# New order tables for a fused RWKV and WaveMLP kernel: r of two pairs loaded first, weight casts in groups of three, all bonus products on GpSimd

## The chip, the cores and the metric

The kernel runs on one core of a Trainium2 chip. The metric is device time in microseconds (us) of one launch, taken as the median of several runs. Beside it stands one profiled execution, from which all durations of single instructions come.

## The reference, cut to what matters

Two stages follow each other. The first is a recurrent attention over 4 batches, 8 heads, 768 tokens and a head size of 48, with a decay `w` and a bonus `u` per head and channel. The second is a mixing block over the 384 channels.

```
for t in range(S):                                # attention, per batch and head
    cur = einsum('bhd,bhe->bhde', u * k_t, v_t)
    y_t = einsum('bhd,bhde->bhe', r_t, state + cur)
    state = w * state + einsum('bhd,bhe->bhde', k_t, v_t)
x = y, heads side by side                         # 4 x 768 x 384
theta = x @ w_theta
z_r, z_i = x * cos(theta), x * sin(theta)
u = x + w_tok_r @ z_r + w_tok_i @ z_i             # over the 768 tokens
out = u + max(u @ w_ch, 0)
```

## The kernel before

The attention is done in pairs of chunks of 128 tokens: 3 pairs per batch, 12 pairs in all, called g0 to g11 here (`g` in the code). The pairs g0 to g6 are loaded token by token in pairs of neighbours (one DMA each for k, r and v), the later ones in two halves for k and v.

For each pair these steps follow each other:

- SP loads k, r and v as float32 (`load`, DMA at L476, halves at L482), into a ring of 16 buffers `ld`.
- The decay products `Kw` and `Rw` (L613, for later pairs L615) multiply k and r with tables of powers of w. The tables are made by ACT at L429 in the opening.
- PE turns both (`flip TK`, `flip TR`, L555), ACT copies them out of PSUM to `KT` and `RT` (L565).
- PE makes the scores (L657). They are masked on the way out: by DVE alone (L667, from a bank), or copied out by ACT (L670) and multiplied by DVE or GpSimd (L667 from SBUF).
- The bonus: `PD` is the product of RT and KT (L683, L685), PE sums it (`diag`, L703), ACT copies the sums out as `dg` (L708), and `yd` = dg x v (L712) is the bonus product. PE adds it to the output (L841), or DVE does (L886) for later pairs. `vb` is v in bf16 (L633 to L637).
- The state: PE's outer products (L736), DVE's sums F and T (L780 to L788), the decay N (L791, L792), copies in bf16 `Sd` or `Sb` (L751 to L760). `states` (L812, L864) and `outputs` (L825, L877) sum up the result, which goes out as `x` (L849, L851, L886).

Then the mixing: PE or a transposing DMA turns x (L531, or L524 on SP), PE multiplies with w_theta (`theta`, L902), ACT takes sine and cosine (L909, L913), DVE multiplies them with x (`z`, L917). With z of a batch's three pairs PE makes the token mix (`mix`, L938, 72 groups of four matmuls), DVE or ACT and GpSimd add x (L947, L949, L954), the sum is turned again, PE multiplies with w_ch (`chan`, L971), and the result is written out (L977, L980, L984, then DMAs at L990 and L995).

The mix needs the two token matrices turned and in bf16. They come through six casting DMAs on GpSimd's queue (`cast`, L496; two blocks of 128 rows each), land in buffers that are used for other things later, and are turned by PE (`flip W`, L531) into `WrT` and `WiT`. Two more casts bring w_theta and w_ch.

The work around the change is ordered by hand-written tables. All steps are listed as tasks, 840 of them. `ORDER` gives the sequence in which they are issued, so the sequence in which each engine finds its own instructions; an engine never passes over one that still waits. `WAYS` has a digit for each task, which chooses among the ways that the task offers (for the bonus product: 0 is GpSimd, 1 is DVE). `BANKS` gives PE tasks their PSUM banks, `AFTER` adds waits between two tasks that need none by their data, `IDLE` adds matmuls whose result nobody reads. The loop that reads them is this:

```
for seq in order:
    t = self.tasks[seq]
    way = t.ways[int(ways[seq])]
    if way[0] == PE:
        for tok in t.acq:
            self.bank_of[tok] = int(next(given))
    out = way[-1]()
    for d in waits.get(seq, ()):
        tc.add_manual_dep(t.ins[0].ins, d.ins[1].ins.name, ...)
```

The bonus product and its two ways:

```
P.add([pool(1432, lambda f=bonus: f(nc.gpsimd)),
       dve(2 * HD, lambda f=bonus: f(nc.vector), port=True)],
      rd=[kd, kv], wr=[ky], prio=pb + 4, name="yd")
```

Of the kernel before, what the change touches and what calls it, by code (L numbers as in the profile page):

```python
# [30 lines left out]
    3, 9, 37, 0, 1, 8, 6, 2, 20, 7, 116, 16, 17, 10, 19, 38, 4, 11, 117, 21, 12, 29, 15, 22, 30,  # L31
    13, 18, 164, 14, 5, 24, 23, 39, 26, 119, 28, 25, 72, 163, 121, 27, 31, 122, 73, 74, 33, 34,
    118, 75, 120, 76, 77, 32, 123, 36, 165, 89, 41, 84, 124, 167, 90, 131, 91, 35, 79, 206, 134,
    126, 136, 129, 135, 170, 78, 127, 130, 171, 87, 252, 128, 93, 85, 137, 166, 88, 80, 82, 94,
    40, 168, 95, 138, 96, 81, 83, 169, 101, 46, 86, 102, 183, 173, 103, 174, 97, 205, 92, 178,
    176, 184, 181, 185, 177, 125, 42, 44, 132, 51, 182, 43, 104, 98, 133, 140, 179, 105, 100, 106,
    99, 141, 180, 142, 107, 143, 144, 56, 172, 139, 207, 148, 149, 45, 150, 108, 145, 151, 175,
    187, 152, 153, 112, 146, 188, 147, 154, 189, 186, 114, 109, 155, 113, 300, 190, 111, 159, 110,
    209, 156, 161, 61, 191, 158, 192, 115, 193, 157, 212, 194, 195, 160, 47, 196, 213, 48, 49,
    299, 197, 341, 50, 255, 198, 201, 162, 199, 257, 200, 346, 202, 203, 342, 253, 204, 347, 54,  # L40
    208, 343, 55, 52, 210, 344, 399, 348, 53, 345, 211, 214, 258, 220, 225, 215, 221, 229, 349,
    59, 223, 226, 230, 350, 351, 60, 224, 232, 57, 227, 352, 218, 365, 58, 219, 231, 366, 233,
    254, 228, 237, 360, 216, 234, 361, 66, 236, 217, 235, 367, 398, 303, 64, 62, 222, 65, 306,
    302, 400, 362, 63, 368, 304, 307, 256, 369, 238, 305, 239, 240, 319, 314, 242, 259, 241, 315,
    320, 260, 243, 363, 402, 316, 301, 309, 321, 244, 364, 267, 312, 262, 310, 370, 270, 245, 268,
    311, 263, 248, 272, 269, 265, 589, 69, 249, 67, 266, 405, 247, 70, 261, 68, 273, 317, 384,
    590, 71, 250, 313, 318, 379, 271, 406, 401, 246, 276, 274, 385, 371, 445, 277, 279, 278, 403,
    264, 275, 380, 404, 284, 407, 418, 444, 386, 280, 281, 419, 308, 381, 251, 282, 422, 420, 387,
    446, 322, 323, 423, 285, 388, 286, 382, 287, 426, 383, 408, 288, 289, 413, 427, 492, 425, 411,
    389, 421, 290, 390, 325, 356, 412, 490, 409, 416, 391, 357, 410, 594, 375, 291, 592, 358, 353,  # L50
    392, 372, 354, 393, 295, 376, 417, 355, 491, 596, 297, 324, 377, 394, 373, 283, 296, 556, 449,
    374, 591, 395, 326, 424, 450, 597, 451, 593, 292, 452, 496, 453, 293, 429, 454, 327, 414, 396,
    430, 328, 294, 329, 415, 456, 466, 330, 331, 431, 432, 457, 461, 332, 433, 551, 464, 434, 458,
    459, 499, 465, 447, 435, 495, 500, 467, 448, 537, 637, 436, 497, 333, 635, 298, 334, 498, 337,
    462, 595, 532, 338, 636, 440, 336, 512, 468, 335, 557, 359, 339, 598, 600, 681, 437, 460, 599,
    463, 570, 441, 340, 682, 513, 455, 533, 494, 641, 439, 538, 442, 438, 539, 469, 514, 534, 443,
    493, 540, 615, 470, 683, 644, 471, 473, 575, 472, 640, 616, 378, 576, 639, 618, 617, 642, 535,
    541, 638, 552, 536, 643, 553, 645, 474, 686, 475, 542, 507, 502, 577, 657, 501, 503, 558, 510,
    428, 504, 397, 505, 571, 511, 559, 572, 506, 687, 508, 560, 516, 601, 517, 509, 476, 554, 477,
    658, 602, 555, 478, 561, 515, 659, 688, 604, 480, 603, 690, 689, 479, 543, 647, 547, 481, 619,  # L60
    648, 650, 544, 646, 691, 548, 651, 518, 573, 549, 606, 605, 661, 578, 609, 574, 562, 519, 545,
    520, 607, 579, 580, 728, 521, 546, 620, 608, 563, 522, 662, 566, 523, 564, 610, 723, 482, 664,
    565, 567, 742, 649, 568, 569, 581, 486, 684, 483, 487, 685, 611, 582, 524, 484, 550, 585, 488,
    665, 525, 485, 583, 663, 747, 586, 489, 584, 527, 528, 612, 587, 529, 729, 530, 748, 588, 613,
    526, 743, 531, 692, 724, 614, 730, 703, 749, 731, 744, 750, 732, 725, 745, 751, 704, 746, 726,
    752, 707, 652, 705, 708, 621, 727, 667, 655, 693, 668, 696, 653, 622, 656, 660, 733, 623, 694,
    766, 625, 654, 669, 624, 767, 695, 670, 626, 761, 671, 706, 762, 753, 672, 768, 734, 763, 666,
    769, 697, 770, 698, 764, 627, 709, 699, 628, 701, 765, 771, 631, 700, 630, 702, 673, 710, 629,
    711, 757, 633, 712, 738, 758, 735, 713, 739, 759, 674, 632, 714, 754, 634, 677, 755, 772, 773,
    679, 756, 804, 678, 774, 675, 776, 736, 740, 775, 676, 715, 799, 737, 680, 741, 785, 760, 716,  # L70
# [968 lines left out]
```

## Time and profile before

| what | value |
|---|---|
| median of 3 runs | 138.47 us (138.37 to 138.68) |
| profiled execution | 139.18 us, of which the span from the first to the last instruction is 137.4 us |
| mean granted TensorE clock | 0.993 |
| PE busy | 127.3 us (93%) in 1779 matmuls |
| DVE busy | 109.8 us (80%) in 215 instructions |
| ACT busy | 80.1 us (58%) in 170 |
| GpSimd busy | 53.4 us (39%) in 61 |
| DMA | 24.87 MB, mean 181 GB/s |

PE is TensorE's matmul, PEld its weight load, DVE is VectorE, ACT ScalarE, POOL GpSimd, SP SyncE. All times in the views are counted from the span's start. A timeline row has the start, the duration, the engine, the line, the operation with output and inputs, and in brackets the engine's idle time before it and what ended that. A row of groups has the count, the busy time, the mean of one in ns, the idle time before them and who ended it. PE's matmuls overlap, so that a row's duration is longer than the time until the next can start.

### The profile page before, as it was taken

The numbers are of one execution on the slowest core, as the hardware profiler recorded it, in microseconds if no ns is written. First come the engines' busy times: TensorE is split into PE (matmuls) and PEld (weight loads), VectorE is DVE, ScalarE is ACT, GpSimd is POOL, SyncE is SP. The second block draws the span as 40 slices with busy tenths as digits, with TensorE's granted clock in tenths as the row PEclk, the third lists the DMA queues.
The fourth block names the chain that finished last, engine by engine and source line by source line (L and its number), as shares of the span: only waits on it lengthen the run. The fifth ranks groups of instructions, "written<-read, shape, count | busy, mean of one in ns | idle before, by whom it ended". The sixth has DMA issues, their size and how long they took to land.

```text
span 137.4 us, 4323 instructions
## 1 busy us (share of the span) xinstructions
PE 127.3 (93%) x1779; PEld 83.4 (61%) x1779; DVE 109.8 (80%) x215; ACT 80.1 (58%) x170; POOL 53.4 (39%) x61
## 2 busy tenths in 40 slices
PE   7887898799999999999989999999999999999870
PEld 2255565576776777666766575766667665566430
DVE  7699998687999999999889977996778587324390
ACT  5587969695555798547858836271954058530110
POOL 6007676510042360394630025989107933212000
PEclk9999999999999999999999999999999999999997
DMA  4999999999999999790089999766952563536344
GB/s 104 271 261 261 230 277 209 210 275 248 255 255 262 200 214 185 154 225 12 0 100 237 266 192 289 188 122 119 256 207 55 117 107 69 216 127 42 77 172 172
DMA packets 64799, 24.87 MB, mean 181 GB/s; under 512 B 59402, under 2 KB 64779, under 8 KB 64779
## 3 DMA queue, kind: packets, MB, share of 16 engines
q1 hardware_dynamic: 62320, 21.63, 71.1%
q0 software_dynamic: 2432, 2.95, 12.5%
q8 instruction: 14, 0.23, 0.7%
q14 instruction: 7, 0.05, 0.1%
q10 hardware_dynamic: 26, 0.00, 0.0%
HBM read 20.06 MB, written 4.72 MB: 180 GB/s over the span
## 4 chain that ended last, share of the span: by engine, by line
PE 64%; DVE 12%; DMA 10%; ACT 6%; issue 3%; SPq 1%; POOL 1%; ACTq 0%; POOLq 0%
PE bank L938 25%; PE bank L902 8%; PE bank L971 8%; PE bank L555 6%; DMA ld<-in_r_dram 4%; PE bank L657 4%; DVE mAT L667 3%; DMA uu_all<-uu_all 3%; PE bank L531 3%; DMA xT<-x 3%; PE bank L825 2%; DVE Rw L613 2%; ACT vb L633 2%; PE bank L877 2%; PE bank L736 2%
## 5 line engine op out<-in xcount | busy, mean ns | idle before, releaser
L938 PE MATMUL bank<-z,WrT 128*128 128x384 bf16 x144 | 46.9, 326 | 0.0
L938 PE MATMUL bank<-z,WiT 128*128 128x384 bf16 x144 | 46.8, 326 | 0.0
L938 PEld LDWEIGHTS <-WiT 128*128 128x128 bf16 x144 | 14.1, 98 | 8.2
L938 PEld LDWEIGHTS <-WrT 128*128 128x128 bf16 x144 | 14.0, 97 | 8.0
L909 ACT ACTIVATE trig<-bank,pi 128x384 f16<-128x384 f32 x24 | 13.9, 587 | 5.5 <-PE bank L902 5.4
L917 DVE TENSOR_TENSOR z<-x,trig 128x1536 bf16<-128x1536 bf16 x12 | 11.5, 955 | 6.3 <-ACT trig L913 3.6
L902 PE MATMUL bank<-Wth,xT 128*128 128x384 bf16 x72 | 14.5, 327 | 1.4 <-DVE Sd L770 1.2
L947 DVE TENSOR_TENSOR uu_all<-bank,x 128x384 bf16<-128x384 f32 x20 | 11.1, 564 | 5.9 <-PE bank L938 5.7
L670 ACT ACTIVATE mAT<-bank 128x512 bf16<-128x512 f32 x20 | 11.1, 597 | 6.3 <-PE bank L657 6.3
L971 PE MATMUL bank<-Wch,uu_all 128*128 128x384 bf16 x72 | 14.0, 327 | 0.7 <-DMA uu_all<-uu_all 0.7
L913 ACT ACTIVATE trig<-bank 128x384 f16<-128x384 f32 x24 | 11.5, 494 | 3.6 <-PE bank L902 3.6
L712 POOL TENSOR_TENSOR yd<-dg,vb 128x768 bf16<-128x768 f32 x7 | 10.3, 1471 | 6.8 <-DVE z L917 6.3
L980 DVE SCALAR_TENSOR_TENSOR fin_all<-bank,uu_all 128x384 f32<-128x384 f32 x19 | 10.2, 551 | 2.1 <-PE bank L971 2.0
L667 DVE TENSOR_TENSOR mAT<-bank,mask 128x512 bf16<-128x512 f32 x17 | 11.2, 683 | 0.1
L565 ACT ACTIVATE KT<-bank 128x512 f32<-128x512 f32 x12 | 7.0, 596 | 6.8 <-PE bank L555 6.8
L613 DVE TENSOR_TENSOR Rw<-ld,rpow 128x768 bf16<-128x768 f32 x10 | 10.1, 1017 | 0.2
L902 PEld LDWEIGHTS <-xT 128*128 128x128 bf16 x72 | 6.7, 98 | 5.4 <-issue 1.1
L971 PEld LDWEIGHTS <-uu_all 128*128 128x128 bf16 x72 | 6.6, 98 | 5.3 <-DMA uu_all<-uu_all 1.0
L984 POOL TENSOR_TENSOR fin_all<-fin_all,uu_all 128x384 f32<-128x384 f32 x5 | 4.6, 930 | 13.0 <-ACT fin_all L977 6.8
L657 PE MATMUL bank<-RT,KT 64*64 64x128 bf16 (+1 forms) x304 | 8.8, 220 | 0.3 <-issue 0.2
L555 PE MATMUL bank<-ident_f,Kw 128*128 128x128 f32 x48 | 7.7, 282 | 1.0 <-DVE Kw L613 0.6
L297 PE MATMUL bank<-zero 128*128 128x512 bf16 x21 | 7.4, 475 | 1.0 <-DVE zero L331 1.0
(125 smaller groups left out, 241.8 us busy)
## 6 DMA issues: line engine op xcount, KB each, us to landing
ld<-in_r_dram SPq DMA_DIRECT2D x12, 384.0 KB, 6.0
out_dram<-fin_all SPq DMA_DIRECT2D x11, 384.0 KB, 3.5
ld<-in_k_dram SPq DMA_DIRECT2D x7, 384.0 KB, 6.3
ld<-in_v_dram SPq DMA_DIRECT2D x7, 384.0 KB, 6.3
ld<-in_k_dram SPq DMA_DIRECT2D x10, 192.0 KB, 5.8
ld<-in_v_dram SPq DMA_DIRECT2D x10, 192.0 KB, 4.2
z<-in_moe_w_tok_r_dram POOLq DMA_DIRECT2D x1, 384.0 KB, 7.9
x<-in_moe_w_tok_i_dram POOLq DMA_DIRECT2D x1, 384.0 KB, 8.8
```

What stands on the lines that cost most here:

```text
L555: ins = [nc.tensor.matmul(bank(tok)[:, i * C:(i + 1) * C], s.bitcast(F32), ident_f, is_transpose=True, start=(i == 0), stop=(i == n - 1)) ...
L613: return eng.tensor_mul(to.rearrange("p h d j -> p h j d")[:, :, :, :D], tokens(i), pw)
L657: ins.append(nc.tensor.matmul(to[:, hp * C:(hp + 1) * C], a, m, start=(hp == 0), stop=(hp == HP - 1), skip_group_check=True))
L667: return eng.tensor_mul(mAT[:, hi], bank(tk[hi]).rearrange("p (h t) -> p h t", h=HP) if src is None else src, bc(m, 1, HP))
L670: act(HP * C, lambda hi=hi, tk=tk, mAT=mAT: nc.scalar.activation(mAT[:, hi], bank(tk[hi]).rearrange("p (h t) -> p h t", h=HP), Act.Copy))],
L902: ins = [nc.tensor.matmul(bank(th)[:, :HD], xt[:, dk], Wth[:, dk, :], start=(dk == 0), stop=(dk == ND - 1)) for dk in range(ND)]
L909: P.add(act(HD, lambda th=th, t=t, g=g: nc.scalar.activation(trig_at(g)[:, t, 0], bank(th)[:, :HD], Act.Sin, bias=pi2), 144), use=[th], rd ...
L913: P.add(act(HD, lambda th=th, t=t, g=g: nc.scalar.activation(trig_at(g)[:, t, 1], bank(th)[:, :HD], Act.Sin)), use=[th], rd=["sin"], wr=[( ...
L917: P.add(dve(4 * HD, lambda g=g: nc.vector.tensor_mul(z_at(g), bc(x_at(g), 2, 2), trig_at(g)), 2.0, True), rd=xk + [("trig", g % 2, t, i) f ...
L938: ins.append(nc.tensor.matmul(bank(tm)[:, :HD], (WrT, WiT)[ri][:, so, to * C:(to + 1) * C], z_at(b * NP + part)[:, i // 2, ri], start=(par ...
L947: P.add([dve(HD, lambda tm=tm, t=t, g=g: nc.vector.tensor_add(un_at(g)[:, t], bank(tm)[:, :HD], x_at(g)[:, t])), act(HD, lambda tm=tm, t=t ...
L971: ins = [nc.tensor.matmul(bank(tf)[:, :HD], ut[:, dk], Wch[:, dk, :], start=(dk == 0), stop=(dk == ND - 1)) for dk in range(ND)]
```

## The change

`ORDER`, `WAYS`, `BANKS`, `AFTER` and `IDLE` are all replaced; nothing else is touched. The work is the same, matmul by matmul, and so are the 21 fillers (10 fixed, 11 in `IDLE`). The new file has one line more ahead of the functions, so that its line numbers are one higher. Of the tables the diff's core is this:

```
 ORDER = [
-    3, 9, 37, 0, 1, 8, 6, 2, 20, 7, 116, 16, 17, 10, 19, 38, 4, 11, 117, 21, 12, 29, 15, 22, 30,
+    2, 3, 38, 0, 4, 6, 16, 7, 18, 117, 8, 9, 116, 19, 1, 10, 37, 21, 20, 29, 14, 22, 12, 30, 17,
...
 AFTER = [
-    (35, 46), (80, 40), (95, 51), (139, 145), (141, 56), (159, 61), (164, 41), (167, 136),
+    (47, 56), (55, 71), (89, 166), (121, 41), (122, 40), (128, 139), (135, 92), (147, 115),
+    (157, 51), (167, 46), (172, 186), (205, 61), (225, 303), (228, 232), (232, 234), (232, 236),
```

In `AFTER` (167, 46) reads: task 46 waits until task 167 is done. The tasks that the text speaks of are 41, 46, 51, 56, 61, 66 (the casts of the token matrices), 40 and 71 (w_theta and w_ch), 92, 139, 186, 228 (bonus products of g0 to g3), 166 (`Kw` of g2), 89 (`PD` of g0), 121 and 122 (`flip TK` of g1 and its copy out), 47 (a flip of the second cast), 157 (a cosine of g1), 205 (the load of k of g3), 167 (`Rw` of g2), 115 (`z` of g0).

By way, over all pairs: the bonus products go from 7 on GpSimd and 5 on DVE to 12 on GpSimd. Mask steps that DVE does in one go from the bank go from 28 to 34, those copied out by ACT first from 20 to 14; of the multiplications behind ACT's copies GpSimd had 9 and DVE 11, now 6 and 8. Decay products on GpSimd go from 3 to 5, `PD` from 3 to 2, N from 4 to 6, copies Sb0 from 3 to 6. Of the turned weights DVE copies out 7 instead of 5 and ACT 5 instead of 7. A memset (`lw0`) goes from DVE to GpSimd. Of the turns of x, six stay on SP's DMA, one of them another pair's (g6 in place of g5).

First place, SP's queue from its start: the loads, by buffer and tensor. ld_90 and ld_93 hold r of g0 and g1, ld_89 and ld_92 k of g0 and g1, ld_96 and ld_95 r and k of g2, ld_91, ld_94 and ld_97 v of g0, g1 and g2. Before:

```order
L476 DMA ld_89<-in_k_dram 128x8x96
L476 DMA ld_92<-in_k_dram 128x8x96
L476 DMA ld_90<-in_r_dram 128x8x96
L476 DMA ld_93<-in_r_dram 128x8x96
L476 DMA ld_96<-in_r_dram 128x8x96
L476 DMA ld_91<-in_v_dram 128x8x96
L476 DMA ld_95<-in_k_dram 128x8x96
L476 DMA ld_94<-in_v_dram 128x8x96
L476 DMA ld_97<-in_v_dram 128x8x96
```

and after the change:

```order
L477 DMA ld_90<-in_r_dram 128x8x96
L477 DMA ld_93<-in_r_dram 128x8x96
L477 DMA ld_92<-in_k_dram 128x8x96
L477 DMA ld_89<-in_k_dram 128x8x96
L477 DMA ld_96<-in_r_dram 128x8x96
L477 DMA ld_95<-in_k_dram 128x8x96
L477 DMA ld_91<-in_v_dram 128x8x96
L477 DMA ld_94<-in_v_dram 128x8x96
L477 DMA ld_97<-in_v_dram 128x8x96
```

Both r loads stand ahead of both k loads, and k of g2 is sixth where it was seventh.

Second place, GpSimd's queue behind its memsets. z_157, x_155, uu_all and fin_all are the landing buffers of the casts; tok_r and tok_i are the two token matrices. Before:

```order
L496 DMA z_157<-in_moe_w_tok_r_dram 128x2x768
L683 TENSOR_TENSOR PD_125<-RT_118,KT_122 128x1024
L496 DMA Wth<-in_moe_w_theta_dram 128x3x384
L496 DMA x_155<-in_moe_w_tok_i_dram 128x2x768
L712 TENSOR_TENSOR yd_150<-dg_147,vb_111 128x768
L496 DMA uu_all<-in_moe_w_tok_r_dram 128x2x768
L759 CAST Sd_144<-N_133 64x4x48 x2
L496 DMA fin_all<-in_moe_w_tok_i_dram 128x2x768
L791 TENSOR_TENSOR N_134<-T_135,w_86 128x192
L667 TENSOR_TENSOR mAT_130<-mAT_130,mask_72 128x512
L712 TENSOR_TENSOR yd_152<-dg_149,vb_113 128x768
L496 DMA fin_all<-in_moe_w_tok_r_dram 128x2x768
```

and after the change:

```order
L497 DMA Wth<-in_moe_w_theta_dram 128x3x384
L614 TENSOR_TENSOR Kw_109<-ld_95,kpow 128x8x2x48
L497 DMA x_155<-in_moe_w_tok_i_dram 128x2x768
L713 TENSOR_TENSOR yd_150<-dg_147,vb_111 128x768
L713 TENSOR_TENSOR yd_151<-dg_148,vb_112 128x768
L792 TENSOR_TENSOR N_134<-T_135,w_86 128x192
L760 CAST Sd_146<-N_134 64x4x48
L713 TENSOR_TENSOR yd_152<-dg_149,vb_113 128x768
L760 CAST Sd_146<-N_134 64x4x48
L497 DMA fin_all<-in_moe_w_tok_i_dram 128x2x768
L497 DMA uu_all<-in_moe_w_tok_r_dram 128x2x768
L497 DMA fin_all<-in_moe_w_tok_r_dram 128x2x768
```

The first cast (z_157) still stands ahead of these rows. The cast of w_theta now follows it directly, a decay product of g2 stands between them and the third cast, and the next three casts follow each other behind all three bonus products of batch 0.

Third place, DVE between the third pair's first masked scores and the second pair's state sums. Before, with the bonus product of g1 (yd_151):

```order
L667 TENSOR_TENSOR mAT_126<-bank_66,mask_72 128x512
L784 TENSOR_TENSOR F_131<-bank_68,N_133 128x192
L760 CAST Sd_145<-F_131 64x4x48
L788 TENSOR_TENSOR T_135<-bank_63,F_131 128x192
L712 TENSOR_TENSOR yd_151<-dg_148,vb_112 128x768
L545 COPY xT_160<-bank_64 128x768
L851 CAST x_153<-bank_62 128x384
```

and after the change, around the same sums:

```order
L668 TENSOR_TENSOR mAT_128<-mAT_128,mask_72 128x512
L785 TENSOR_TENSOR F_131<-bank_66,N_133 128x192
L789 TENSOR_TENSOR T_135<-bank_63,F_131 128x192
L668 TENSOR_TENSOR mAT_126<-bank_61,mask_72 128x512
L546 COPY WrT<-bank_62 128x6x128
L668 TENSOR_TENSOR mAT_126<-bank_67,mask_72 128x512
L668 TENSOR_TENSOR mAT_130<-bank_65,mask_72 128x512
```

The bonus product, the copy of F, the copy of the turned x and the copy out of x have left this stretch for GpSimd and ACT; a turned weight and a mask step have come in.

More of the change, by code (lines that the diff above doesn't have):

```diff
@@ L30 @@
 ORDER = [
[44 rows of a table removed]
[44 rows of a table added]
 ]
 WAYS = (
-    "000000000000000000000000000001100000000000000000100001010000100000000010000000001212"
-    "012000000012001110000000100000000000000000000000000010010020000000001001000000000000"
-    "000000110000000000000000000101000000000000000010000001211000101200022000000010000000"
-    "000000000201212000120001000201000000010100000000000000000000120000000000000000101200"
-    "000000000000000000110110000000000000011011000000000000001100000000100000000000001100"
-    "000100000000000010000000000000000000000120120010010000100000012000000000000000000000"
@@ L84 @@
-    "000000000000000000012000000000000000111101101100000000000110110110000000000011011000"
-    "000000100000100011011110001001000000001200000000000000000020110000000100000001100000"
-    "120000000000000100000011110120000000000000120000000000110001111011000000000000001100"
-    "001100000000000110110000000000001111011011000000000001101101100000000000000110000110"
+    "001000000000000000000000000001100000000000010000001001000000100101001000000000000000"
+    "000000000010001200000000000000000000000000012000121200000000001100000001000000000010"
@@ new lines @@
+    "000010000000000000000000000101000000000000000000001200000000000020001000010000000000"
+    "000000000001100000110000000000120000000100000000000100000011000000000000000000010100"
+    "000000000000000000110110000000000000011011000011000000001101100000000000000000000000"
+    "000000011000010120000000000000000000000000000010000000010000012000000000000010000000"
+    "011000000000000000012000000000000000001101101100000000000110000000000000000011011011"
+    "000000000000001200000121000011000000001200000000000010000020001100000000000000000000"
@@ L88 @@
+    "120000000000001000000012120001100000000000120000000000110000011011011000000000111101"
+    "100000000000000110000000000110000011011011000000000001101100000000000000000110000110"
 )
 BANKS = (
-    "012345670213564715175206145271472310567234015762134057623471620354603514271462730165"
-    "270361526413502715376145026547206453726076123560731601276072673621676174265617254176"
-    "20365741326413213604752161324075613274610574632064751306"
+    "012345670214365701270542370652173152071364521037641025761025726035267142360174530123"
@@ L94 @@
+    "570463270546327046123716267053276405124671250476410075314571602537150264354263714063"
+    "57134062157653223124430712354760124536724531064306247150"
 )
 AFTER = [
[4 rows of a table removed]
[5 rows of a table added]
 ]
 IDLE = [
-    (74, 6, 2), (76, 7, 2), (84, 1, 1), (137, 2, 3), (140, 3, 3),
+    (76, 5, 1), (123, 6, 2), (121, 7, 1), (74, 0, 1), (90, 7, 3), (93, 4, 1), (173, 3, 2),
 ]
```

92 rows, old and new, of tables (AFTER, ORDER) are left out of this document.

## The prediction

> **What bounds the kernel now.** I read the busy time by stage first (all windows of the span). Columns: length in us, then busy time of PE, of its weight load, of DVE, ACT and GpSimd with their instructions, the granted clock, the DMA engines' share, GB/s.
>
> ```profile
> 0.00:25.00 25.00, 20.60 (x352) 12.14 (x353) 21.77 (x63) 18.69 (x36) 12.40 (x24) 1.00 1.13 230
> 25.00:36.00 11.00, 11.00 (x133) 7.78 (x132) 8.88 (x13) 7.29 (x16) 1.65 (x2) 1.00 1.16 252
> 36.00:66.00 30.00, 29.63 (x537) 21.04 (x536) 29.61 (x57) 21.15 (x46) 12.04 (x11) 1.00 0.89 187
> 66.00:92.00 26.00, 25.45 (x392) 17.32 (x391) 22.82 (x39) 16.03 (x36) 12.06 (x10) 1.00 0.92 183
> 92.00:124.50 32.50, 32.50 (x328) 20.64 (x325) 21.19 (x37) 15.95 (x37) 15.07 (x16) 1.00 0.55 135
> 124.50:133.40 8.90, 8.12 (x52) 4.45 (x50) 4.94 (x9) 0.98 (x2) 0.23 (x1) 1.00 0.56 108
> 133.40:137.40 4.00, 0.00 (x0) 0.00 (x0) 0.56 (x1) 0.00 (x0) 0.00 (x0) 0.78 0.43 158
> ```
>
> From 25 to 124.5 PE is busy for 98.6 of 99.5 us: TensorE sets the pace, and its matmuls are the same after the change. What can be won there is 0.9 us. The last 4.0 us hold only the last sums and stores. The place where PE stands is the opening: 4.4 us idle of 25, part of the busy rest being matmuls that nobody reads. There DVE has 21.77 us of work. It has 29.61 of 30.00 in the third window too, so it is the engine that could let PE wait in the middle.
>
> The opening is therefore the stage to read closely. DVE's timeline, whose fields are start and duration in us, engine, line, operation, count and the idle time before:
>
> ```profile
> 5.96 1.93 DVE L613 TENSOR_TENSOR Kw<-ld,kpow 128x768 bf16<-128x768 f32 x2 [1.05 <-ACT kpow L429]
> 7.78 2.18 DVE L613 TENSOR_TENSOR Rw<-ld,rpow 128x768 bf16<-128x768 f32 x2
> ...
> 10.41 0.69 DVE L683 TENSOR_TENSOR PD<-RT,KT 128x1024 bf16<-128x1024 bf16 x1
> 11.02 1.02 DVE L613 TENSOR_TENSOR Rw<-ld,rpow 128x768 bf16<-128x768 f32 x1
> 12.08 2.48 DVE L667 TENSOR_TENSOR mAT<-bank,mask 128x512 bf16<-128x512 f32 x4
> ```
>
> The last of the first four products waits for its load. In the chain of waits, r of g1, the fourth load, is the release:
>
> ```profile
> 2.89 6.03 DMA ld<-in_r_dram
> 8.94 1.02 DVE Rw L613
> ```
>
> GpSimd's queue in the same stage:
>
> ```profile
> 10.74 0.90 POOL L496 DMA_DIRECT2D z<-in_moe_w_tok_r_dram  x1 [7.99 <-DMA ld<-in_r_dram]
> 12.21 2.12 POOL L683 TENSOR_TENSOR PD<-RT,KT 128x1024 bf16<-128x1024 bf16 x1 [0.57 <-DVE Rw L613]
> 15.67 0.80 POOL L496 DMA_DIRECT2D Wth<-in_moe_w_theta_dram  x1 [1.34 <-ACT mAT L670]
> 16.47 0.74 POOL L496 DMA_DIRECT2D x<-in_moe_w_tok_i_dram  x1
> 17.75 1.46 POOL L712 TENSOR_TENSOR yd<-dg,vb 128x768 bf16<-128x768 f32 x1 [0.54 <-DVE PD L683]
> 19.17 0.76 POOL L496 DMA_DIRECT2D uu_all<-in_moe_w_tok_r_dram  x1
> 20.29 0.74 POOL L759 CAST Sd<-N 64x192 bf16<-64x192 f32 x2 [0.36 <-DVE N L792]
> 21.57 0.72 POOL L496 DMA_DIRECT2D fin_all<-in_moe_w_tok_i_dram  x1 [0.55 <-DVE Sd L760]
> ```
>
> And PE, from the first bonus sum to the first matmul of the token mix:
>
> ```profile
> 19.46 0.50 PE L841 MATMUL bank<-yd,place 64*128 64x384 bf16 x4
> ...
> 22.74 0.50 PE L841 MATMUL bank<-yd,place 64*128 64x384 bf16 x4
> ...
> 24.77 0.65 PE L902 MATMUL bank<-Wth,xT 128*128 128x384 bf16 x3 [1.17 <-DVE Sd L770]
> ...
> 28.32 0.66 PE L555 MATMUL bank<-ident_f,Rw 128*128 128x128 f32 x4
> 28.81 1.17 PE L531 MATMUL bank<-ident,x 128*128 128x128 bf16 x18
> 29.82 0.33 PE L938 MATMUL bank<-z,WrT 128*128 128x384 bf16 x1
> ```
>
> The bonus sum of g0 starts as soon as GpSimd's product is done, 17.75 + 1.46 = 19.21. GpSimd could not begin it earlier, since two casts stand ahead and DVE's `PD` holds it for another 0.54. From the first theta (24.77) to the first mix (29.82) PE is practically never idle. So the start of the mix hangs on the bonus chain of g0 and g1, and what comes behind runs at PE's pace. An earlier mix is worth its full time as long as nothing behind it starts to starve.
>
> **The change part by part: the opening.** I walk the new order with the durations above. A place without a row of its own takes that of the same operation.
>
> Loads and products. The two r products take the place of the two k products at 5.96 (the r tables are now made first), 0.97 each, until 7.9. k of g1 runs until 9.0. k of g0 is now the fourth load; it lands at 2.89 + 6.03 = 8.92 as the fourth did, and its product ends at 10.0, as before. r of g2 is the fifth load in both and its product ends about 11.5 instead of 12.04. But both `PD` now stand on DVE behind it, so the mask steps begin at about 12.7 instead of 12.08: 0.6 lost here, and GpSimd is freed of its `PD` of 2.12. It uses that for the k product of g2, with 1.83 by the row below, 12.75 to 14.6, where DVE had it behind four masks (12.08 + 2.48 = 14.56) and until about 15.5. Swapping r and k by itself is worth nothing, since four products are needed in any case and the fourth load ends them.
>
> Three rows price the ways that are exchanged: the bonus product on both engines (min/median/max in ns, then first and last start), and from the groups the r product on GpSimd.
>
> ```profile
> L712 POOL TENSOR_TENSOR yd<-dg,vb x7: 1463/1471/1484, 17.7 to 108.4; 128x768 bf16<-128x768 f32 x7
> L712 DVE TENSOR_TENSOR yd<-dg,vb x5: 940/951/957, 21.7 to 101.3; 128x768 bf16<-128x768 f32 x5
> ```
>
> ```profile
> L613 POOL TENSOR_TENSOR Rw<-ld,rpow 128x768 bf16<-128x768 f32 x2 | 3.7, 1828 | 4.8 <-PE bank L555 4.8
> ```
>
> Bonus products. On GpSimd the cast of w_theta goes out right behind the first cast, at about 10.5. That leaves, behind the k product, one cast of 0.74 ahead of the bonus product of g0, which runs from about 15.85 to 17.3. PE's bonus sum of g0 comes at 17.5 instead of 19.46. That of g1, whose product now runs on GpSimd at 19.2 to 20.7 beside DVE's steps from PSUM, comes at 21.0 instead of 22.74. It takes 1.47 instead of 0.95, yet DVE has its 0.94 free at 21.7, in the very stretch that leads to the state copies for which theta waits (1.17). The first theta then starts at about 21.4 and the first mix at 26.05 instead of 29.82, 3.77 earlier. Two turns that PE did ahead of the mix now come behind it, the one of r at 28.32 (0.49 until the next start) and that of x of g2, a third of the 18 matmuls from 28.81 to 29.82 (0.34): 3.77 - 0.83 = 2.94 us. It fits into the 4.4 that PE idles there.
>
> The other moves in the opening I take at nothing. Copies of turned x go to ACT, which idles 6.3 of the 25 us. The memset goes to GpSimd, where no row shows it: 0 from below, and from above 0.5 (an estimate: were it as long as GpSimd's longest step above, 2.12, it would delay the tables for which DVE waits at 5.96 by about that). I take 0, since they also wait for other things.
>
> **The grouped casts.** Here the change adds waits: the casts 56, 51 and 61 wait for a flip of the second cast, for a cosine of g1 and for the load of k of g3. By my walk they are issued at about 24.4, 25.5 and 26.5. Queued behind them on GpSimd are the r product of g5, a mask step and the cast of w_ch; all casts' time from issue to landing, and three of them one by one:
>
> ```profile
> DMA to landing us min/median/max: 6.3/8.0/8.8
> ```
>
> ```profile
> x<-in_moe_w_tok_i_dram POOLq DMA_DIRECT2D x1, 384.0 KB, 8.8
> uu_all<-in_moe_w_tok_r_dram POOLq DMA_DIRECT2D x1, 384.0 KB, 8.4
> fin_all<-in_moe_w_tok_i_dram POOLq DMA_DIRECT2D x1, 384.0 KB, 8.5
> ```
>
> With the issues of 16.47, 19.17 and 21.57 these three landed at 25.3, 27.6 and 30.1, about 2.4 apart: casts close together drain one after the other. PE's flips of the three groups stand 7.0, 9.3 and 11.5 us of its work behind the first mix, so at 33.1, 35.3 and 37.5. With 8.4 and 2.4 the casts land at 32.8, 35.2 and 37.6; with the longest 8.8 at 33.2, 35.6 and 38.0, which is 0.5 late. I take +0.5. Before, the two of them that land in uu_all and fin_all first were asked for at 19.17 and 21.57, 6.3 and 2.8 us earlier, and PE did not wait (second window): this cover is what the grouping spends. From below the cost is 0. From above: the widest gap between two landings of before is from the first cast (10.74 + 7.9 in its issue row, 18.6) to w_theta (15.67 + 7.2, 22.9), 4.3 us. With that gap the third would land at 32.8 + 8.6 = 41.4, 3.9 late.
>
> **Middle and end.** DVE gives up five bonus products of 0.95 and two decay products of about 1.0; mask steps, copies and sums go both ways and nearly cancel. That is about 7 us of its 109.8 in the span, and GpSimd takes about 8 on its 53.4. In the third window that loosens DVE (29.61 of 30.00), but PE lost only 0.37 there and 0.55 in the fourth window. Between a gain of 0.9 and a loss by products that now take 1.47 on the path, I take 0. The bound for the loss comes from this row, in which DVE waits for GpSimd:
>
> ```profile
> 96.09 1.23 DVE L685 TENSOR_TENSOR PD<-RT,KT 128x1024 bf16<-128x1024 bf16 x1 [1.16 <-POOL mAT L667]
> ```
>
> A product of two operands in SBUF on DVE did not start until GpSimd's was done; so did GpSimd's bonus product at 17.75, by 0.54. In all of the trace no such pair overlaps, while DVE's steps from PSUM run on. So a GpSimd product of 1.47 can cost DVE's next product at most 1.47. [...]
>
> The stores and the last mixing steps keep their ways, 0.
>
> **The sum.** -2.94 + 0.5 + 0 = -2.44. The profiled execution took 139.18 (span 137.4 and 1.78 around it), so 136.7 for the same kind of run; it lay 0.71 above the median of 138.47, and the medians give about 136.0.
>
> **The rivals.**
>
> More than that: DVE, lighter by 7 us, also removes PE's 0.9 in the middle, and the casts land in time. -2.94 - 0.92 = -3.86, 134.6. For it speaks that DVE leads into PE's waits of 36 to 66; against it that some of the waits there are for a DMA turn of x, which stays.
>
> [...]
>
> The gain is given back: PE starts the mix earlier, but with loads and casts drawn from the same queue at 230 to 252 GB/s in both first windows it only meets the next wait earlier; 138.4, no change. Against it: in the second window PE was never idle, so the loads had some lead.
>
> Slower: the casts in a group starve. If SP's loads, in full flow until 36, take turns with three casts at once, the third lands at 41.4 and PE stands at the flips of its group: -2.94 + 3.9 = +0.96, 139.4. It decides from a landing at 37.5 + 2.94 = 40.4 on. For it speaks the gap of 4.3; against it that in that gap the cast behind was itself issued 4.9 after the first, and that the backlogged ones came 2.4 apart. [...]
>
> That the change does not do what it says is not a rival: the order of the built program shows every move named here.
>
> **How the numbers follow.** My forecast has 0.53: 136.0, its own range 135.0 to 137.2. More than that has 0.14, the shared port 0.11, the gain given back 0.09, the starving casts 0.13. A difference below 0.2% (138.19 to 138.75) could not be told from no change. The first three are faster, 0.78 together. The given-back case straddles that band: 0.01 of it counts as faster, 0.07 as the same, 0.01 as slower. So 0.79, 0.07 and, with the starving casts, 0.14. The range that holds 8 in 10 goes from 134.2, 0.4 below the larger gain, to 138.6, so that it leaves out the slower rival and a little on the low side.
>
> **What would show it.** Right: the first mix near 26, bonus sums of g0 and g1 near 17.5 and 21, first theta near 21.4; GpSimd's first bonus product starting near 15.9; the three casts landing no later than 38; PE busy for all but a few tenths from the first mix to 90; DVE's busy time near 103. Wrong: a first mix after 28 (a product held by the other engine, to be seen as a DVE wait released by POOL or the reverse), or PE idle at flips of the weights between 33 and 41 with a cast as the release, or a load of k or r landing late behind the casts.

## The result, and the profile after

The changed kernel takes 137.48 us (17 runs), the kernel before 138.72 in the same comparison: a ratio of 0.989, interval 0.986 to 0.992, so 1.5 us (1.1 to 1.9) faster. Runs in the chip's slower state stay out of all ratios here, among them three of these 17 and four of e3's six. Forecast were 136.0 and a gain of 2.44. The direction was right and the range of 134.2 to 138.6 held (the main case's own, 135.0 to 137.2, was missed by 0.3), but the gain did not come from where the working had put it.

The profiled execution took 137.24 us. Its windows, with the last cuts set 1.9 us earlier than before:

```profile
0.00:25.00 25.00, 20.45 (x348) 12.13 (x349) 20.29 (x60) 19.15 (x40) 11.42 (x22) 1.00 1.12 231
25.00:36.00 11.00, 10.10 (x155) 7.29 (x155) 9.38 (x14) 7.83 (x17) 3.12 (x5) 1.00 1.11 235
36.00:66.00 30.00, 30.00 (x561) 22.32 (x560) 26.18 (x48) 19.57 (x42) 19.19 (x17) 1.00 0.91 198
66.00:92.00 26.00, 25.77 (x350) 17.94 (x349) 23.41 (x41) 14.94 (x33) 13.01 (x12) 1.00 1.12 191
92.00:122.60 30.60, 29.53 (x316) 18.34 (x315) 19.62 (x33) 16.30 (x37) 12.79 (x14) 1.00 0.50 131
122.60:131.50 8.90, 8.72 (x57) 4.98 (x55) 4.92 (x9) 1.97 (x4) 1.83 (x2) 1.00 0.35 91
131.50:135.50 4.00, 0.00 (x0) 0.00 (x0) 0.56 (x1) 0.00 (x0) 0.00 (x0) 0.95 0.53 195
```

The opening, forecast as the place of the gain, idles as before (4.55 of 25 us against 4.40) and passes 0.90 more into the second window. The third and fourth windows lose 0.23 instead of 0.92, and DVE there is no longer full (26.18 of 30 against 29.61). A new idle us stands in the fifth.

PE's timeline of the opening shows what happened. The rows are the bonus sums of g0 and g1, the first theta, the turn of x of g1, the outer products of g2 in two pieces, and the first mix:

```profile
18.20 0.48 PE L842 MATMUL bank<-yd,place 64*128 64x384 bf16 x4
...
22.11 0.48 PE L842 MATMUL bank<-yd,place 64*128 64x384 bf16 x4
22.53 1.15 PE L903 MATMUL bank<-Wth,xT 128*128 128x384 bf16 x6
23.51 0.50 PE L532 MATMUL bank<-ident,x 128*128 128x128 bf16 x6
24.01 0.21 PE L737 MATMUL bank<-vb,Kw 64*64 64x48 bf16 x2
25.91 0.40 PE L737 MATMUL bank<-vb,Kw 64*64 64x48 bf16 x14 [1.68 <-issue]
...
29.16 0.34 PE L939 MATMUL bank<-z,WrT 128*128 128x384 bf16 x1
```

The walk held to within 1.1 us up to the first theta (18.2, 22.1 and 22.5 against 17.5, 21.0 and 21.4). Then PE stands for 1.9 us in the middle of a group of like matmuls, after 2 of 16, released by "issue", which is nothing that the profile's waits show.

The page's table of DMA queues names what could: a queue that carries instructions.

```profile
q8 instruction: 14, 0.23, 0.7%
```

These are 14 transfers of 16 KB each. PE has 3581 instructions in the trace, 3558 of them matmuls and weight loads, which is close to 14 times 256; no other engine has more than 270. The count alone proves little, since e5, with 128 more, has 14 transfers too. The places say more. Counting PE's instructions from zero, the stall stands exactly ahead of the 705th, and a smaller one (18.69 to 19.29) ahead of the 449th, 256 earlier. The 193rd, another 256 earlier, is where PE enters the block ahead of these two; the blocks that begin at 193, 449 and 705 are called the first, second and third here. The transfers end at 17.77 and 24.51; PE goes on 1.5 and 1.4 us later. The kernel before has the same two stalls at the same counts: transfers end at 16.87 and 23.38, PE goes on at 18.30 and 24.77. The second is the wait of 1.17 that its profile puts down to DVE's state copies.

### The profile page after: what moved, and what is told of

It reads as the page before. It is cut to its first block, busy times and chain, and to the rows that moved or that the text cites. A ratio compares the mean times of both kernels' runs of the same rounds, so it can differ in the third digit from the quotient of the medians.

```text
span 135.5 us, 4313 instructions
## 1 busy us (share of the span) xinstructions
PE 124.6 (92%) x1779; PEld 83.0 (61%) x1779; DVE 104.4 (77%) x203; ACT 79.8 (59%) x168; POOL 61.4 (45%) x70
## 3 DMA queue, kind: packets, MB, share of 16 engines
q1 hardware_dynamic: 62320, 21.63, 73.1%
q0 software_dynamic: 2432, 2.95, 12.4%
HBM read 20.06 MB, written 4.72 MB: 183 GB/s over the span
## 4 chain that ended last, share of the span: by engine, by line
PE 80%; DMA 6%; DVE 5%; issue 2%; ACT 2%; POOL 1%; DVEq 0%
PE bank L939 35%; PE bank L903 8%; PE bank L556 7%; PE bank L972 6%; PE bank L532 5%; PE bank L658 4%; DMA uu_all<-uu_all 3%; DMA xT<-x 3%; PE bank L737 3%; PE bank L826 3%; PE bank L298 2%; DVE Rw L614 2%; PE bank L842 2%; PE bank L813 2%; PE bank L704 1%
## 5 line engine op out<-in xcount | busy, mean ns | idle before, releaser
L713 POOL TENSOR_TENSOR yd<-dg,vb 128x768 bf16<-128x768 f32 x12 | 17.6, 1474 | 5.6 <-DVE vb L636 1.9
L910 ACT ACTIVATE trig<-bank,pi 128x384 f16<-128x384 f32 x24 | 13.4, 584 | 2.8 <-PE bank L903 2.8
L903 PE MATMUL bank<-Wth,xT 128*128 128x384 bf16 x72 | 14.0, 326 | 0.2 <-DMA xT<-x 0.2
L668 DVE TENSOR_TENSOR mAT<-bank,mask 128x512 bf16<-128x512 f32 x21 | 13.5, 680 | 0.0
L955 POOL TENSOR_TENSOR uu_all<-fin_all,x 128x384 bf16<-128x384 f32 x4 | 3.7, 918 | 19.6 <-issue 7.9
L981 DVE SCALAR_TENSOR_TENSOR fin_all<-bank,uu_all 128x384 f32<-128x384 f32 x18 | 9.6, 551 | 2.2 <-PE bank L972 2.1
L668 DVE TENSOR_TENSOR mAT<-bank,mask_c 128x512 bf16<-128x512 f32 x13 | 8.8, 684 | 1.6 <-PE bank L658 1.6
L985 POOL TENSOR_TENSOR fin_all<-fin_all,uu_all 128x384 f32<-128x384 f32 x6 | 5.4, 912 | 9.4 <-ACT fin_all L978 9.4
L566 ACT ACTIVATE RT<-bank 128x512 f32<-128x512 f32 x12 | 7.2, 600 | 3.2 <-PE bank L556 3.2
```

The source lines that it names most:

```text
L566: ways = [act(n * C, lambda: nc.scalar.activation(dst.bitcast(F32), bank(tok)[:, :n * C], Act.Copy))]
L668: return eng.tensor_mul(mAT[:, hi], bank(tk[hi]).rearrange("p (h t) -> p h t", h=HP) if src is None else src, bc(m, 1, HP))
L713: return eng.tensor_mul(yd.rearrange("p a b d -> p (a b) d"), wide(dg, D), vb.rearrange("p a b d -> p (a b) d"))
L903: ins = [nc.tensor.matmul(bank(th)[:, :HD], xt[:, dk], Wth[:, dk, :], start=(dk == 0), stop=(dk == ND - 1)) for dk in range(ND)]
L910: P.add(act(HD, lambda th=th, t=t, g=g: nc.scalar.activation(trig_at(g)[:, t, 0], bank(th)[:, :HD], Act.Sin, bias=pi2), 144), use=[th], rd ...
```

## The experiments

Theory 1: PE's instructions come in blocks of 256, and in the opening PE uses them up faster than they arrive. Theory 2: what holds PE there is data, as in the prediction. Ratios are to the kernel before, in runs on the same chip. The changed kernel was not run again beside the experiments, so a comparison with it goes through two ratios, and its ratio of 0.989 and an experiment's can differ by the chip, too.

**e1_no_fillers.**

```diff
-IDLE = [(76, 5, 1), (123, 6, 2), (121, 7, 1), (74, 0, 1), (90, 7, 3), (93, 4, 1), (173, 3, 2)]
+IDLE = []
```

> The changed kernel without the 11 matmuls of IDLE that nobody reads (22 instructions of PE fewer in the opening). Theory 1 (PE's instructions come in blocks of 256, and in the opening a block comes about 6.5 us after PE entered the one before; the boundaries are PE's instructions 193, 449, 705): the stall of 1.9 us at 24.0 stays, but moves on by 11 pairs of instructions, so that it no longer stands after 2 of the 16 outer products of g2 but after about 13; it again ends near 26, first mix near 29.1 (28.8 to 29.4), the time within 0.4% of the changed kernel. Theory 2 (PE waits there for data, above all for v of g2 in bf16, which DVE made at 23.4 to 24.0): the stall stays at the same outer product or goes, and the first mix comes up to 1 us earlier.

Measured: no stall left at that count, since PE is later: it reaches the 705th instruction at 25.24, and the block's transfer ended at 23.64, so by the 1.4 us above the block was there at 25.0. First mix at 28.32. The granted clock is 0.50 from 15.8 to 22.6, where the changed kernel has 1.00: so the fillers keep the clock. The whole is slower than the changed kernel, 138.49 us, ratio 0.997 (0.995 to 0.999), but that the clock costs this is not shown. The first mix comes 0.84 earlier in spite of it, behind it the clock is 1.00, and the profile's largest new wait of PE stands near the end:

```profile
129.99 1.15 PE L999 MATMUL bank<-Wch,uu_all 128*128 128x384 bf16 x6 [1.36 <-DMA uu_all<-uu_all]
```

The place of the stall could not be tested.

**e2_loads_held.**

```diff
 ORDER: tasks 252 and 205 (loads of k of g4 and g3) moved from ahead of task 104 to right behind it
 AFTER = [
+    (104, 252),
```

> The changed kernel, in which SP's load of k of g4, and so all loads behind it, waits for PE's bonus sum of g0 (about 18.2). Theory 1, with the 4 us between PE's entry into a block and the start of the next block's transfer put down to the loads and casts in flight: the transfer that started at 16.8 starts by 15, the stalls at 18.7 and 24.0 shrink to under 0.5 together, and the first mix comes at 26.5 to 27.5 instead of 29.2; the whole is 0 to 2 us faster, less what the later loads cost in front of the turns of g3 and g4. Theory 2: the stall at 24.0 stays as it is (1.9 us), first mix not before 28.8, and the whole is equal or slower by what the loads come later.

Measured: 135.38 us, ratio 0.976 (0.974 to 0.978), the fastest kernel of the study, and faster than the changed one by 1.3% (0.976 / 0.989). PE's timeline of e2 at the same place, and its windows:

```profile
23.37 0.21 PE L772 MATMUL bank<-vb,Kw 64*64 64x48 bf16 x2
24.17 0.40 PE L772 MATMUL bank<-vb,Kw 64*64 64x48 bf16 x14 [0.59 <-issue]
...
27.43 0.34 PE L974 MATMUL bank<-z,WrT 128*128 128x384 bf16 x1
```

```profile
25.00:36.00 11.00, 11.00 (x168) 7.96 (x166) 10.82 (x17) 9.04 (x19) 3.52 (x5) 1.00 1.12 232
36.00:66.00 30.00, 30.00 (x539) 21.89 (x538) 26.17 (x48) 19.56 (x42) 18.21 (x17) 1.00 0.94 212
66.00:92.00 26.00, 25.78 (x361) 17.93 (x360) 22.60 (x39) 14.98 (x33) 14.70 (x14) 1.00 1.09 186
92.00:121.50 29.50, 29.45 (x311) 18.16 (x304) 19.16 (x32) 15.02 (x34) 11.96 (x13) 1.00 0.47 126
```

The stall stands at the same matmul and has shrunk from 1.9 to 0.8; the first mix comes 1.73 earlier, of which some 0.35 is there by the 193rd instruction already and not the hold's (e3, the same as the changed kernel up to the first mix, is 0.38 earlier there too: two executions of one opening differ by that much). The two stalls together are 1.1 us, not under 0.5. DVE's part has not changed, so theory 2 falls. The third block was asked for at 18.65 (when PE entered the second) and its transfer started at 21.73, after 3.1 us instead of 4.0. That the transfer of the second block would start by 15 was wrong: it started at 16.33.

**e8_held_longer.**

```diff
 ORDER: tasks 252, 205, 253 and 206 (loads of k and r of g4 and g3) moved to right behind task 112
 AFTER = [
+    (112, 252),
```

> The changed kernel with the same hold as e2, but until PE's second theta of g0 (about 22.5). Theory 1: the transfer of the third block, asked for near 18.6 with only casts in flight, starts by 20.8 (16.3, 21.7 in e2), the stall at the 705th instruction is gone, and the first mix comes at 26.3 to 27.0 (27.4 in e2); but k of g4 and g3 come later, PE waits at their turns, and the whole lies between e2 and 1 us slower than e2. If loads in flight have nothing to do with the block's arrival: the stall of 0.8 stays and the first mix is at 27.2 or later.

Measured: asked for at 19.11, the third block's transfer started at 21.01, after 1.9 us, and the stall at the 705th instruction is gone; the first mix is at 27.13, just outside what was expected. The whole is 142.86 us, ratio 1.029 (1.025 to 1.034), far worse than expected, since the loads are too late. DVE's timeline has the one that costs it, and PE stands for 4.9 us behind it:

```profile
38.02 1.02 DVE L649 TENSOR_TENSOR Rw<-ld,rpow 128x768 bf16<-128x768 f32 x1 [5.18 <-DMA ld<-in_r_dram]
```

**e11_held_shorter.**

```diff
 ORDER: tasks 252 and 205 moved to right behind task 93
 AFTER = [
+    (93, 252),
```

> The changed kernel with the hold of e2, but only until PE's outer products of g0 (about 16.2), so some 2 us shorter. Theory 1: the third block is asked for near 18.6 with more loads in flight than in e2, and comes between 24.2 (e2) and 25.9 (changed kernel), first mix at 27.5 to 28.8; the loads of k and r of g3 and g4 come earlier than in e2, so that the whole lies within 0.8 us of e2, more likely above it.

Measured: released at 16.2, the loads are in flight again when the block is asked for (19.21). Its transfer starts at 23.09, 3.9 us later, the stall is 1.89 long and the first mix is at 29.09, as without a hold and not as expected. 136.41 us, 1.0 above e2, ratio 0.981 (0.977 to 0.985).

**e5_more_short.**

```diff
 IDLE = [
+    (5, 2, 64),
...
+        if wide == 0:
+            ins = [nc.tensor.matmul(bank_t[k][:, :16], zero, zero[:, :16], start=True, stop=True,
+                                    skip_group_check=True) for i in range(n)]
```

> The changed kernel with 64 more unread matmuls, 16 columns wide, directly behind the fixed fillers at about 6, where PE is idle until 7.9: 128 instructions more, some 2 us that fall into idle time. Theory 1 (blocks of 256 instructions of PE): the boundaries now fall 128 of the old instructions earlier, the block behind the old 577th instruction comes near 24 and that behind the old 833rd near 30.4, so that PE stands longer and the first mix starts at 30.3 to 31.5 instead of 29.2; the kernel is 0.8 to 2.4 us slower than the changed one. Theory 2 (PE waits for data): idle time is filled, first mix 28.8 to 29.4, same time within 0.4%.

Measured: first mix at 30.16, ratio 1.0245 (1.019 to 1.030), 142.1 us: slower by more than expected, though the first mix is not. PE's timeline:

```profile
20.08 0.55 PE L571 MATMUL bank<-ident,z 128*128 128x128 bf16 x7
22.39 0.45 PE L571 MATMUL bank<-ident,z 128*128 128x128 bf16 x5 [1.75 <-issue]
...
24.55 2.06 PE L942 MATMUL bank<-Wth,xT 128*128 128x384 bf16 x6
```

With 128 instructions more, all in time in which PE had been idle, the stall has moved to other work, a turn of weights, and stands again ahead of the 705th instruction. Behind it six theta matmuls take 2.06 us instead of 1.15, at a granted clock of 0.50 from 23.0 to 26.4. In e3 the clock is 0.50 from 26.3 to 29.7, behind an idle stretch of 1.69, and six theta matmuls take 2.13; in the profiles of the changed kernel and of e11 the same stall, with idle stretches of 1.68 and 1.69, passes at 1.00. A stall of this length thus can cost twice, and does not always; in e5 the clock fell behind a gap of 1.75 us. Of the 4.4 us by which e5's span is longer than the changed kernel's, 1.0 is there at the first mix and 1.0 is one more stall of this kind, ahead of the 1729th instruction (50.90 to 51.91). The rest is not explained; two waits for DVE, of 1.13 and 1.34 us, stand behind 110.

**e7_before_held.**

```diff
 (of the kernel before) ORDER: tasks 206, 252 and 205 moved to right behind task 104
 AFTER = [
+    (104, 206),
```

> The kernel before, in which SP's load of r of g3, and so all loads behind it, waits for PE's bonus sum of g0 (about 19.4); nothing else changed. Theory 1: the block of PE's instructions behind the 705th comes earlier than 24.8 (its transfer started at 22.4), first mix 28.3 to 29.2 instead of 29.8, and the whole 0.4 to 1.5 us faster if the later loads still come in time. Theory 2 (PE's wait at 23.5 to 24.8 is for DVE's state copies): first mix within 0.2 of 29.8, whole equal or slower.

Measured: the block comes 1 us earlier (23.81 instead of 24.77), but the first mix only 0.25 (29.57): PE now idles 0.32 ahead of a turn at 27.75, for a decay product of DVE, and spends 0.32 more in the turns behind it. Ratio 1.002 (0.998 to 1.005). In the order of before, relieving the block is worth nothing.

**e4_bonus_only** and **e3_bonus_back** test the bonus products.

```diff
 (of the kernel before) WAYS of tasks 139, 228, 275, 469, 614 (bonus products)
-    1 1 1 1 1
+    0 0 0 0 0
```

> The kernel before with all five bonus products of DVE moved to GpSimd and nothing else changed. If DVE's relief is the gain: 0.8 to 2 us faster than the kernel before, the first mix still near 29.8, since the opening is bound by something else. If the bonus product of g1 on DVE bound the opening, as the prediction had it, the first mix comes 0.5 us or more earlier. If GpSimd products of 1.47 us in place of 0.95 cost DVE and PE as much as they relieve: no change or slower.

Measured: slower, 139.97 us, ratio 1.0077 (1.006 to 1.010), first mix at 29.75. Its third and fourth window and the first of PE's waits:

```profile
36.00:66.00 30.00, 28.88 (x533) 20.47 (x531) 29.60 (x55) 20.40 (x45) 14.94 (x13) 1.00 0.93 187
66.00:92.00 26.00, 25.06 (x369) 17.01 (x367) 22.01 (x37) 16.24 (x36) 12.40 (x10) 1.00 0.89 177
```

```profile
PE bank L866 <- POOL yd L737: 1.2, 1, 1.2
```

DVE's third window is as full as before (29.60): what it is rid of, it spends otherwise, and PE waits more (2.06 us idle in the two windows, before 0.92).

```diff
 (of the changed kernel) WAYS of tasks 228, 275, 469, 614
-    0 0 0 0
+    1 1 1 1
```

> The changed kernel with four of the five moved bonus products, those of g3, g4, g7 and g9, back on DVE; that of g1 stays on GpSimd. If the gain of the change comes from DVE's relief between 36 and 92 us: 0.8 to 2.4 us slower than the changed kernel, and PE's idle time between 36 and 92 grows from 0.2 to 1 us or more. If it comes from the order of loads and casts: within 0.4 us of the changed kernel.

Measured: ratio 0.989 (0.985 to 0.992), the same as the changed kernel's, but from two runs, 136.86 and 137.77 us; the median of all six is 139.15. The profile, of a run of 139.34, has the sign that was named for DVE's relief: PE idles 1.30 us between 36 and 92, not 0.23. Two of its waits there and just behind are for DVE, 1.11 together; one of 0.62 is for a turning DMA.

```profile
36.00:66.00 30.00, 29.32 (x579) 21.66 (x581) 27.44 (x50) 19.10 (x40) 14.72 (x15) 1.00 0.85 185
66.00:92.00 26.00, 25.38 (x326) 17.26 (x313) 23.25 (x41) 14.98 (x33) 11.47 (x10) 1.00 1.15 191
```

```profile
48.06 0.34 PE L847 MATMUL bank<-Sd,RT 128*128 128x96 bf16 x4 [0.68 <-DVE Sd L795]
...
96.66 0.38 PE L692 MATMUL bank<-RT,KT 64*128 64x128 bf16 x7 [0.43 <-DVE mAT L702]
```

PE's instructions stand in the same order in both kernels. From the first mix (30.18) to the matmul at 96.66 e3's PE takes 66.5 us, the changed kernel's 64.5 for the same instructions, both at a granted clock of 1.00. In e2, e11 and e12 it is 64.4 to 64.7. So in the new order the four products on GpSimd save PE up to 2 us by this one trace. The run times neither confirm nor exclude it. In the old order moving all five alone loses (e4).

**e10_casts_early** undoes two thirds of the grouping.

```diff
 ORDER: task 56 moved to right behind task 92, task 51 to right behind task 139
 AFTER = [
-    (47, 56),
-    (157, 51),
```

> The changed kernel with the grouping of the casts undone for two of the three: cast 56 is asked for right behind the bonus product of g0 (about 18.1), cast 51 behind that of g1 (about 21.3), without their waits; before the group stood at 27.4 to 29.7. Theory 1 with transfers in flight as what delays the block of PE's instructions: the block behind the 705th comes later than 25.9, first mix at 29.4 to 30.4, the whole 0.2 to 1.2 us slower than the changed kernel. If the casts in flight don't matter for it: first mix 28.9 to 29.3 and the whole within 0.4 us of the changed kernel; the flips of the weights do not wait in either case.

Measured: ratio 0.983 (0.978 to 0.988), first mix at 28.69, the third block's transfer 4.1 us after it was asked for: two casts more in flight between 18 and 24 do not delay it further. The first mix is earlier than either case had it, by no more than e3's unaltered opening differs. No cost of the early casts shows.

**e12_k_first.**

```diff
 ORDER, BANKS, IDLE, AFTER: exchanged (38, 37), (117, 116), (73, 72), (120, 119), (76, 74), (123, 121), (77, 75), (124, 122), (25, 23), (26, 24), (20, 19)
```

> The changed kernel with r and k of g0 and g1 exchanged back in the opening: loads, tables, products, turns and copies of k stand where those of r stood, and the reverse. Since the fourth load ends the four products in both, and PE's count of instructions is the same: first mix at 28.8 to 29.5, the whole within 0.4 us of the changed kernel. If r first is what gains: slower by 0.5 us or more.

Measured: first mix at 28.72, ratio 0.982 (0.978 to 0.985), lower than the changed kernel's, so outside of what was expected, and not slower: no sign that r first earns anything. That the reverse earns something is not shown either. e10 and e11, run beside it, have 0.983 and 0.981, and a first mix 0.44 earlier lies within what e3's unaltered opening shows (its 705th instruction is 0.55 earlier).

**e6_old_opening** and **e9_new_opening** join the two orders at the first mix.

```diff
 e6: ORDER, WAYS, BANKS, IDLE and AFTER of before for all tasks ahead of its first mix (341), of the changed kernel for the rest
 e9: of the changed kernel for all tasks ahead of its first mix (346), of before for the rest
```

> Order, ways and banks of the kernel before up to its first matmul of the token mix, and from there those of the changed kernel for all that is left. If the gain of the change lies behind the first mix: ratio to the kernel before 0.983 to 0.995, as the changed kernel has it, with the first mix near 29.8 and PE idle for under 0.5 us between 36 and 92. If it lies in the opening (loads of r first, casts, bonus products of the first three pairs): ratio 0.996 to 1.004.

> The counterpart of e6: order, ways and banks of the changed kernel up to its first matmul of the token mix, and from there those of the kernel before. The early loads of the changed kernel bring k and r of g3 and g4 in time here. If the gain lies behind the first mix: ratio to the kernel before 0.996 to 1.006, first mix near 29.2, PE idle between 36 and 92 near 0.9 us as before. If it lies in what the opening leaves behind (loads that stand further ahead, the weights turned later): ratio 0.984 to 0.993.

Measured: 143.86 us, ratio 1.037 (1.033 to 1.041), and 142.0 us, ratio 1.024 (1.020 to 1.027). Neither half works with the other: in e6 PE stands for 4.7 us ahead of 39.4, since the load of r that the new order turns next comes late in the old order of loads; in e9 it waits 1.7 at two turns and 1.3 for a cast. They do not tell where the gain lies.

All stalls at the 705th instruction obey one rule. The end of the third block's transfer, and the start of that instruction:

| kernel | transfer asked, start, end | 705th |
|---|---|---|
| before | 18.30, 22.44, 23.38 | 24.77 |
| changed | 19.29, 23.32, 24.51 | 25.91 |
| e2 | 18.65, 21.73, 22.81 | 24.17 |
| e3 | 18.75, 22.79, 23.98 | 25.36 |
| e5 | 16.27, 20.06, 21.11 | 22.38 |
| e6 | 17.77, 21.95, 22.90 | 24.34 |
| e7 | 17.89, 21.54, 22.49 | 23.81 |
| e9 | 19.98, 23.80, 24.94 | 26.32 |
| e10 | 19.10, 23.17, 24.10 | 25.43 |
| e11 | 19.21, 23.09, 24.32 | 25.83 |
| e12 | 18.84, 22.87, 23.93 | 25.46 |
| e8, no stall | 19.11, 21.01, 21.97 | 23.86 |

Wherever PE stands there, it goes on 1.3 to 1.5 us after the transfer's end; in e8 it comes later than that. "Asked" is PE's entry into the block before, an inference that does not fit everywhere. In e5 the transfer of the second block starts 0.2 us after PE's entry into the first (10.94 and 11.14), where the changed kernel has 4.1, and later in the changed kernel two transfers start 0.4 and 0.75 ahead of such an entry (56.29 and 56.72, 62.70 and 63.45).

## Why the prediction came out as it did

**The opening, -2.94 forecast, about +0.2 found.** The step that failed is "the start of the mix hangs on the bonus chain of g0 and g1, and what comes behind runs at PE's pace". In its place the runs showed that it hangs on the third block of PE's instructions, without which PE cannot pass the 705th (25.91). The bonus sums came 1.3 and 0.6 us earlier than before, yet the first mix only 0.66 (29.16), with 0.83 of turns put off behind it: net 0.17 lost. PE even enters the first of these blocks later (12.73 against 11.94; 12.35 in e3, with the same opening), since the k products started at 8.88 and not at the walk's 7.9, waiting for ACT, and each further block takes 6.4 to 6.6 us from there:

```profile
8.88 1.92 DVE L614 TENSOR_TENSOR Kw<-ld,kpow 128x768 bf16<-128x768 f32 x2 [0.31 <-ACT kpow L430]
```

e2, e5 and e8 move this stall by loads and by counts of instructions, with DVE's and GpSimd's work unchanged. The wait of 1.17 for "DVE Sd" in the profile of before was the clue that was read wrongly: a releaser that is named is the last event seen, not proof. The working also had a slip: from its theta at 21.4, the 5.05 us to the mix less the 0.83 of turns that moved give 25.62, not 26.05, so by its own rows the term would have been -3.37.

**The grouped casts, +0.5 forecast, 0 found.** GpSimd's rows and the times to landing:

```profile
27.39 0.77 POOL L497 DMA_DIRECT2D fin_all<-in_moe_w_tok_i_dram  x1 [1.40 <-PE bank L532]
28.98 0.72 POOL L497 DMA_DIRECT2D uu_all<-in_moe_w_tok_r_dram  x1 [0.82 <-ACT trig L910]
29.69 0.72 POOL L497 DMA_DIRECT2D fin_all<-in_moe_w_tok_r_dram  x1
```

```profile
fin_all<-in_moe_w_tok_i_dram POOLq DMA_DIRECT2D x1, 384.0 KB, 6.9
uu_all<-in_moe_w_tok_r_dram POOLq DMA_DIRECT2D x1, 384.0 KB, 7.7
fin_all<-in_moe_w_tok_r_dram POOLq DMA_DIRECT2D x1, 384.0 KB, 9.4
```

They land at 34.3, 36.7 and 39.1, 2.4 apart as worked out, and PE's first turns of them start at 36.3, 38.7 and 40.8. With the mix 3 us later than walked, the cover is 1.7 us or more. Even e2, with its mix at 27.43, has no idle time from 25 to 66.

**Middle and end, 0 forecast, about -2.7 and +0.6 found.** From the first mix to its last matmul PE took 103.6 us before (29.82 to 133.4) and 102.3 now (29.16 to 131.5), although 0.83 of turns have moved in and one stall is new:

```profile
112.40 0.66 PE L972 MATMUL bank<-Wch,uu_all 128*128 128x384 bf16 x3 [1.07 <-DMA uu_all<-uu_all]
```

There a turning DMA took 4.3 us to land instead of the median of 2.8; e11 has the same stall, e2, e10 and e12 do not. The wait of 0.66 for the same kind of DMA at 129 is gone. So the rest of this stretch gave 1.24 + 0.83 + 1.25 - 0.66 = 2.66 us (1.25 from the last start ahead of that stall to the next): small waits for decay products, masks and a turn of x. This is the middle term of the rival "more than that", which I had at 0.14, but at 0.92 of visible idle time it was too small: a matmul's row is longer than the time to the next start, so short waits hide in busy time (the six theta matmuls at 22.53 above have a row of 1.15, and the next row starts after 0.98). Which moves bring it is settled only in part. By e3's one trace up to 2.0 us of it hang on the four bonus products that DVE is rid of, as that rival had it; by e4 the move gains nothing without the rest of the new order. r first (e12) and the grouping (e10) show no part in it. Not tried alone are the masks that DVE takes straight from the bank, the two decay products on GpSimd, the other copies, and the sequence; e6 and e9, which should have told, failed over their loads.

**The rival that the prediction calls the shared port**, with 0.11, had products of DVE and GpSimd hold each other up. That the two share a port is not shown by any run; what the profiles show are waits, before the change of 0.54 and 1.16 us, and in the opening after it none that cost DVE: GpSimd's bonus products of g1 and g2 waited for DVE's results, 1.75 and 1.88 us, and no DVE step of the opening waited for GpSimd.

**The rest of the gap.** Ten of the 14 runs behind the changed kernel's ratio have a mean granted clock of 0.982 to 0.987 and took 136.9 to 137.7; the four at 0.995 or above took 135.8 to 137.2. One stretch of 3.4 us at half the clock, as e5 has it, takes 0.5 x 3.4 / 135.5 = 0.013 off the mean, so the ten fit one such stretch each. e10 and e12, with stalls of 1.6 instead of 1.9, stay at 0.99 or above in nine of ten such runs and take 135.9 and 136.0 in the median. But e11, with a stall of 1.89 in its profile, does so in three of four and takes 136.2. So whether the stall's length or the chip of those runs decides on the clock is open.

**The slower rival** (casts starve) and the one that gives the gain back did not occur. The latter took loads and casts as drawn from the same queue; the page lists a queue q0 with 2.95 MB, which is what the eight casts move (six of 384 KB, two of 288), apart from q1 with 21.63. That the forecast of 2.44 lies near the 2.7 of the middle, and not far from the measured 1.5, is luck: the term that was to bring the gain brought none, and one taken as 0 brought it.

## What to carry to other kernels

Count the instructions of an engine that issues thousands of short ones. Here, with the loads in full flow, PE used up the 256 from 19.29 in 4.7 us, and the next block let it go on after 6.6. There an earlier supply of data did not help (bonus sums 1.3 and 0.6 us earlier, the 705th instruction 1.1 later than before), and 64 small unread matmuls in idle time put the first mix 1.0 us back (e5). A stall in the middle of a group of like matmuls, released by nothing, at the same count in two kernels, is the sign. Holding back loads that are not needed yet while a block is due brought the mix some 1.4 us earlier and made the kernel 1.8 us faster (e2 against the changed one, by their ratios); held back some 4 us longer, the same loads made it 7.5 us slower than that.

## What the runs showed of the hardware that was not expected

- The opening pays 0.6 and 1.9 us for two blocks of instructions, of 256 by the counts at which PE stands and by the 14 transfers of 16 KB for its 3581. From the fourth block on the wait is hidden by 1.4 us or more in the changed kernel, but not in all: in e10 PE stands 1.26 at its 1473rd instruction, which starts 1.3 us after a transfer's end, and in e5 at its 1729th.
- The wait from PE's entry into a block to the start of the next transfer was 4.0 us with loads in flight, 3.1 in e2, 1.9 in e8 and, for the second block, 0.2 in e5. What in the DMA queues holds it back is open: holding the loads shortens it, two more casts do not lengthen it (4.1 in e10).
- Eleven unread matmuls keep the clock: without them it was 0.50 from 15.8 to 22.6 (e1). The kernel lost 1.0 us, although its first mix came 0.84 earlier; that the clock is the cause is not shown.
